# The same 13,990 operations of a two-layer transformer kernel in another written-out order

## The chip, the cores and the metric

The kernel runs on one core of a Trainium2 chip. Its metric is the device time of one execution in microseconds (us); lower is better. Five engines work side by side, each through its own instruction stream: TensorE (in profiles PE for the matmuls and PEld for the weight loads, which are instructions of the same stream), VectorE (DVE), ScalarE (ACT), GpSimd (POOL) and SyncE (SP). POOL and SP do little but issue transfers here. An engine takes its instructions in the order in which they stand in its stream, and semaphores make one engine wait for another.

## The reference

Four blocks follow one another on an input x of 2048 rows by 512 columns, in bf16: A, B, A, B, each added to x after a layer norm.

```
for s in range(64):                       # block A, segments of 32 rows
    h = concat(mem, x[32*s : 32*s+32])    # 8 memory rows + 32 rows
    q, k, v = h @ Wq, h @ Wk, h @ Wv      # 32 heads of 128
    p = softmax(mask(q @ k.T * scale))
    o = (p @ v) @ Wo
    mem = o[:8]                           # the next segment's memory
    outs.append(o[8:])

q, k, v = x @ wqkv                        # block B, linear attention, 32 heads of 16
kv, z = phi(k).T @ v, sum(phi(k))         # over all 2048 rows
out = (phi(q) @ kv) / (phi(q) @ z + 1e-6) @ wo
```

The 64 segments of block A can't run side by side: the memory rows that leave one segment enter the next. What doesn't depend on the memory (the rows' own output, the residual sums, all of block B's input side) can be done at any time after its inputs are there.

## The kernel before

Weights stay on the chip for the whole run. TensorE works with its array cut into four column strips of 32, so that nearly every step is a group of four matmuls, one a strip, and each of the four has its own weight load of 128 x 32. A group can do without the loads when the same weights are still in place; the helper `again` (its instruction is L2077) issues such matmuls.

One segment s of layer l is written as these steps, the names being the third part of the keys in the table:

- `kq0`, `kq1`: keys and queries of 16 heads each (`project`, matmuls of 512 columns at L2191 and L2077). Each result is copied out of PSUM by ACT or DVE (`evac`, L1954 and L1955) and turned by a DVE transpose (L2210).
- `v`: values, the same matmuls, copied out without a transpose.
- `mem0`, `mem1`: attention of the 8 memory rows, for 16 heads each. Number 0 and 1 are the score matmuls (L2325, L2317), 2 and 3 exponentials on ACT (L2332, L2336), 4 a product on DVE (L2340), 5 the matmuls of probabilities with values (L2353), then a reciprocal (L2358), a scaling (L2368 or L2370) and a transpose (L2360) on DVE and ACT.
- `out`: eight times eight matmuls of 256 columns with Wo (L2446), a copy on ACT or DVE (L1954, L1955), a sum on DVE (L2458).
- `next`: small f32 matmuls (L2476) that turn the eight new memory rows, and a copy into the next segment's input. `next` to `kq`, to `mem`, to `out`, to the next `next` is the recurrence that runs through all 64 segments.
- `x`: attention of the 32 rows (products at L2384, matmuls at L2396 and L2416), off that recurrence. `res`: the residual, with its transfers between partitions (`rows_out`). Every fourth segment adds `prep` (layer norm of the next 128 rows), `left` work for eight rows of each segment, `bi` (block B's input side) and, in layer 1, `bo` (the output side of the first block B, L2089). `lq` and `bl` are block B's queries and outputs at the two layers' ends.

What sets the order is a table, not the source's sequence of calls. Every operation has a key: layer, segment, step, number. `PLACE` (lines 16 to 1555) holds for each key one number, and a letter where ACT (`a`) or DVE (`v`) is chosen for an operation that either may do. `schedule` (L1681) sorts all operations by that number:

```
for nd in self.nodes:
    nd.t, nd.eng = when(nd.key, nd.engs)
seq = sorted(self.nodes, key=lambda n: (n.t, n.idx))
```

An engine's stream is the operations of that engine in the sorted order. PSUM banks are dealt out in the same order (the bank whose last user lies furthest back), and `finalize` (L1718) derives the semaphore waits; a wait rides on its instruction, and only an operation that needs two gets a further wait instruction ahead of it. So a change of the numbers alone changes the streams' order, the choice of ACT or DVE, the banks and the waits. The numbers are fixed in the file; the search that made them is not part of it. 

The program's TensorE stream has 43,597 matmuls and 39,357 weight loads. Instructions reach the engine by transfers of their own, on a queue that the profile lists as an instruction queue.

Of the kernel before, what the change touches and what calls it, by code (L numbers as in the profile page):

```python
# [16 lines left out]
    (0, -9, 'setup'): '3 0 1 4 5 7 8 9 10 11 12 13 14 0 6 2 15 16 18 19 20 21 23 26 30 33 36 41 43 45 49 0 59 0 68 100 101 94 99 104 190 212v 48 63a 0 108 113 117 121 126 92 258 0 0 0 0 0 0 0 0 0 0 0 0 0 0 0 0 0 0 0 0 0 0 0 0 0 0 0 0 0 0 0 0 0 0 0 0 0 0 0 0 0 0 0 0 0 0 0 0 0 0 0 0 0 0 0 0 0 0 0 0 0 0 0 0 0 0 0 0 0 0 0 0 0 0 0 0 0 0 0 0 0 0 0 0 0 80 88 0 0 0 0 0 0 0 0 0 0 0 0 0 0 0 0 0 0 0 0 0 0 0 0 0 0 0 0 0 0 0 0 0 0 0 0 0 0 0 0 0 0 0 0 0 0 0 0 0 0 0 0 0 0 0 0 0 0 0 0 0 0 0 0 0 0 0 0 0 0 0 0 0 0 0 0 0 0 0 0 0 0 0 0 0 0 0 0 0 0 0 0 55 0 0 62 0 0 72 84',  # L17
    (0, -5, 'ones'): '131 138 145 148',
    (0, -4, 'start'): '65a',
    (0, -3, 'spin'): '25 27 32 34 37 40 42 44',  # L20
    (0, -2, 'leftv'): '206 210 211 214 217v 222 226 225a 231 237',
    (0, -2, 'prep'): '24 28 29 31 38 46 50a 75v 93a 90v 91v',
    (0, -2, 'prepl'): '35 39 51 53 56 70 73v',
    (0, -1, 'spin'): '83 86 89 97',
    (0, 0, 'kq0'): '116 118 120 125 129 135 137 146 174v 181 159v 179',
    (0, 0, 'kq1'): '111 112 114 115 164 166 167 169 130a 194 172a 176a 187',
    (0, 0, 'ldqkv'): '281',
    (0, 0, 'lq'): '6434 6454 6456 6463 6470 6574 6583 6590',
    (0, 0, 'lx'): '6359',
    (0, 0, 'mem0'): '189 195 204 207 215 238 240 241v 246',  # L30
    (0, 0, 'mem1'): '193 197 203 208 224 247 252 254v 256',
    (0, 0, 'next'): '272 273 278v',
    (0, 0, 'out'): '251 253 255 257 259 261 263 265 268a 286',
    (0, 0, 'ql'): '186v 192a',
    (0, 0, 'sk'): '64 66 67 69 77v 82',
    (0, 0, 'sq'): '144 152 155 156 161a 165',
    (0, 0, 'v'): '218 227 228 230 234a 216 219 220 221 229a',
    (0, 0, 'x'): '233 262 242 249 250 264 266v 284 270 274 276 283 295v 322 243 275 317 356a 429',
    (0, 0, 'xl'): '22',
    (0, 1, 'kq0'): '282 285 287 288 290v 302 291a 298',  # L40
    (0, 1, 'kq1'): '289 293 294 296 292 297 300 301 299a 306 308a 304a 312',
    (0, 1, 'ldqkv'): '370',
    (0, 1, 'lq'): '6429 6451 6524 6527 6551 6556 6561 6582',
    (0, 1, 'mem0'): '309 310 314 336 318 325 328 329v 331',
    (0, 1, 'mem1'): '319 320 324 339 326 330 333 334a 338',
    (0, 1, 'next'): '359 360 361v',
    (0, 1, 'out'): '332 335 337 340 342 343 345 346 351a 358',
    (0, 1, 'ql'): '277a 269v',
    (0, 1, 'res'): '366 362',
    (0, 1, 'sk'): '76 78 79 81 85v 87',  # L50
    (0, 1, 'sq'): '133 134 154 158 168v 184',
    (0, 1, 'v'): '303 305 307 311 316a 313 315 321 323 327a',
    (0, 1, 'x'): '341 344 348 352 353 363 367a 375 354 355 357 372 378a 410 349 350 438 447a 457',
    (0, 2, 'kq0'): '365 369 373 381 383a 389 384v 392',
    (0, 2, 'kq1'): '376 379 380 382 385 386 387 390 388a 396 397a 393a 401',
    (0, 2, 'ldqkv'): '453',
    (0, 2, 'leftv'): '200 202 223 239 245a 260 279 271a 347 364',
    (0, 2, 'lq'): '6749 6761 6764 6765 6775 6787 6789 6797',
    (0, 2, 'lx'): '6433',
    (0, 2, 'mem0'): '398 399 403 427 406 413 416 417v 419',  # L60
    (0, 2, 'mem1'): '407 408 412 424 414 418 421 422a 426',
    (0, 2, 'next'): '448 449 451v',
    (0, 2, 'out'): '420 423 425 428 431 433 434 436 442a 474',
    (0, 2, 'prep'): '47 52 54 57 58 60 61a 98v 171v 140a 142a',
    (0, 2, 'ql'): '371v 377v',
    (0, 2, 'res'): '483 479',
    (0, 2, 'sk'): '74 122 123 124 127a 132',
    (0, 2, 'sq'): '173 178 183 185 188a 196',
    (0, 2, 'v'): '391 394 395 400 405a 402 404 409 411 415a',
    (0, 2, 'x'): '432 435 440 441 450 452 455v 459 444 445 446 458 461v 499 437 443 464 470a 525',  # L70
    (0, 3, 'kq0'): '454 456 460 462 465a 478 466v 472',
    (0, 3, 'kq1'): '463 467 475 477 468 469 471 473 484a 490 481a 476a 486',
    (0, 3, 'ldqkv'): '551',
    (0, 3, 'lq'): '6663 6666 6667 6672 6679 6697 6708 6717',
    (0, 3, 'mem0'): '487 488 493 511 496 502 505 506v 510',
    (0, 3, 'mem1'): '491 497 501 507 503 509 513 516a 520',
    (0, 3, 'next'): '536 538 542v',
    (0, 3, 'out'): '512 517 519 521 523 524 526 527 532a 535',
    (0, 3, 'ql'): '439v 430a',
    (0, 3, 'res'): '546 543',  # L80
    (0, 3, 'sk'): '71 95 96 128 136a 141',
    (0, 3, 'sq'): '139 143 162 177 198a 199',
    (0, 3, 'v'): '480 482 485 489 494a 492 495 498 500 504a',
    (0, 3, 'x'): '515 522 529 531 533 547 549v 552 528 530 540 554 556v 570 539 541 544 548a 589',
    (0, 4, 'kq0'): '545 550 553 555 558v 566 559a 563',
    (0, 4, 'kq1'): '557 564 567 569 560 561 562 565 574a 580 568a 572a 576',
    (0, 4, 'lq'): '6743 6751 6800 6821 6908 6934 6936 6941',
    (0, 4, 'lx'): '6689',
    (0, 4, 'mem0'): '577 578 582 605 585 592 597 599v 602',
    (0, 4, 'mem1'): '586 587 591 603 594 604 608 610v 613',  # L90
    (0, 4, 'next'): '628 629 632v',
    (0, 4, 'out'): '609 611 612 615 616 618 619 620 623a 627',
    (0, 4, 'ql'): '508v 534a',
    (0, 4, 'res'): '670 634 593 596 598 601 606 622 626 630 637a 641 646 644 658 650 662 656 651 663 705',
    (0, 4, 'sk'): '102 103 105 106 147v 149',
    (0, 4, 'sq'): '163 170 180 182 201a 205',
    (0, 4, 'v'): '571 573 575 579 584a 581 583 588 590 595a',
    (0, 4, 'x'): '617 614 625 633 635 640 643v 648 621 631 638 647 652v 673 624 636 716 720a 743',
    (0, 4, 'xl'): '17',
    (0, 5, 'kq0'): '639 642 645 649 657v 664 654a 669',  # L100
    (0, 5, 'kq1'): '661 666 667 671 653 655 659 660 674a 682 665a 668a 677',
    (0, 5, 'lq'): '6818 6848 6863 6866 6912 6919 6921 6927',
    (0, 5, 'mem0'): '675 676 683 680 691 696 702 704a 708',
    (0, 5, 'mem1'): '688 689 693 695 697 706 709 711v 714',
    (0, 5, 'next'): '736 737 739a',
    (0, 5, 'out'): '710 713 715 718 721 722 723 727 730a 740',
    (0, 5, 'ql'): '607a 600a',
    (0, 5, 'res'): '748 751',
    (0, 5, 'sk'): '107 109 110 119 153v 157',
    (0, 5, 'sq'): '150 151 160 175 209v 213',  # L110
    (0, 5, 'v'): '672 679 681 684 687a 678 686 690 692 699a',
    (0, 5, 'x'): '685 726 700 701 703 717 729v 745 731 732 735 786 794v 806 698 733 747 772a 876',
    (0, 6, 'bi'): '719 725 728 734 738 741 712 774 793 799 807 824 842 845 830a 1048 1106 1053 1174 817 822 828 838',
    (0, 6, 'kq0'): '742 746 750 758 761a 766 762v 770',
    (0, 6, 'kq1'): '765 769 771 773 754 768 777 779 776a 781 791a 787a 797',
    (0, 6, 'leftv'): '232 235 244 267 707a 749 752 753a 757 759',
    (0, 6, 'lq'): '6806 6808 6814 6816 6820 6832 6834 6842',
    (0, 6, 'lx'): '6740',
    (0, 6, 'mem0'): '788 792 798 800 801 805 808 810a 814',
    (0, 6, 'mem1'): '803 804 809 836 811 816 819 821a 825',  # L120
    (0, 6, 'next'): '843 844 847a',
    (0, 6, 'out'): '818 820 823 826 829 831 832 835 839a 849',
    (0, 6, 'prep'): '191 236 248 280 368 374 0 724v 518a 514v 537a',
    (0, 6, 'ql'): '780v 694v',
    (0, 6, 'res'): '854 852',
    (0, 6, 'v'): '760 783 784 789 795a 755 756 763 764 767a',
    (0, 6, 'x'): '802 840 812 813 815 827 858v 862 865 866 877 886 889v 899 919 927 931 934a 947',
    (0, 7, 'kq0'): '850 855 857 859 863a 881 868a 872',
    (0, 7, 'kq1'): '875 880 890 891 861 864 870 871 895a 902 874a 879a 883',
    (0, 7, 'lq'): '6798 6801 6803 6850 6918 6929 6930 6937',  # L130
    (0, 7, 'mem0'): '887 888 900 901 905 909 911 913a 917',
    (0, 7, 'mem1'): '896 908 912 921 915 918 922 924v 926',
    (0, 7, 'next'): '944 945 951v',
# [2806 lines left out]
```

## Time and profile before

| | us |
|---|---|
| median of three runs | 1510.44 |
| lowest and highest run | 1507.72, 1513.22 |
| the profiled execution | 1513.92 |
| its span | 1512.0 |
| mean granted TensorE clock | 0.998 |

The profile is of one execution; its span runs from the first to the last instruction, and the execution's time lies 1.9 us above it. Busy times are in us with their share of the span. A matmul's recorded end is modelled and includes the pipeline's tail, so that neighbouring matmuls overlap in the records, and a stream without holes shows in the distance between starts. In lists of waits a row says who waited for whom, then the sum, the number of waits and the longest; "issue" stands for idle time before an instruction that waited for nothing that the profile shows. In the chain of work that ended last, a row gives start, length and what ran.

### The profile page before, as it was taken

What the parts mean: (1) busy time and instruction counts of PE and PEld (TensorE: products, weight loads), DVE (VectorE), ACT (ScalarE), POOL (GpSimd) and SP (SyncE); (2) the same over time, 40 slices, a digit from 0 to 9 for tenths busy, and PEclk for the clock granted to TensorE, in tenths of its full rate; (3) what the DMA queues carried; (4) which work ended last, traced back from release to release, by engine and by line L of the source; (5) the groups of instructions that cost most, each with busy time, mean ns of one, the idle gap of its engine ahead of it and who ended that gap; (6) DMA issues with size and microseconds to landing.
All of it is one profiled execution on the core that took longest, in us unless ns stands there. A gap on an engine that the chain in (4) does not pass through costs nothing.

```text
span 1512.0 us, 90803 instructions
## 1 busy us (share of the span) xinstructions
PE 1458.4 (96%) x43597; PEld 835.8 (55%) x39357; DVE 1227.5 (81%) x4035; ACT 934.3 (62%) x2686; POOL 199.5 (13%) x398
## 2 busy tenths in 40 slices
PE   7999999999999999999999999999999999999998
PEld 3455555555565555555545555555555555555554
DVE  4788888888888788788878888788887888887777
ACT  2566556665665656565566767666666755666656
POOL 3011110111111011111111110111111011111010
PEclk9999999999999999999999999999999999999999
DMA  9310100100000010001310101011110111011034
GB/s 390 106 35 21 35 14 23 25 24 24 25 21 11 23 25 24 25 23 32 64 25 21 28 18 27 25 28 28 25 22 20 26 24 28 20 28 32 16 49 134
DMA packets 81639, 60.26 MB, mean 40 GB/s; under 512 B 64040, under 2 KB 74600, under 8 KB 79720
## 3 DMA queue, kind: packets, MB, share of 16 engines
q1 hardware_dynamic: 67944, 37.58, 9.7%
q0 software_dynamic: 13152, 16.75, 4.0%
q8 instruction: 324, 5.31, 1.5%
q14 instruction: 59, 0.48, 0.1%
q10 hardware_dynamic: 160, 0.14, 0.0%
HBM read 25.57 MB, written 11.67 MB: 25 GB/s over the span
## 4 chain that ended last, share of the span: by engine, by line
PE 81%; DVE 8%; DMA 5%; ACT 3%; issue 1%; SPq 1%; POOL 0%; DVEq 0%
PE pb L2191 36%; PE pb L2446 18%; PE pb L2077 13%; PE pb L2089 3%; PE pb L2396 2%; PE pb L2633 2%; DMA dx_sb<-y_sb 2%; PE pb L2353 2%; PE pb L2416 2%; ACT arena_sb L1954 2%; PE pb L2317 1%; PE pb L2476 1%; DVE arena_sb L2210 1%; DVE arena_sb L1955 1%; DMA Wk_sb<-in_A_Wk_dram 1%
## 5 line engine op out<-in xcount | busy, mean ns | idle before, releaser
L1954 ACT ACTIVATE arena_sb<-pb 128x512 bf16<-128x512 f32 (+3 forms) x1021 | 512.0, 529 | 285.7 <-PE pb L2077 125.5
L2191 PE MATMUL pb<-Wk_sb,arena_sb 128*32 128x512 bf16 x4192 | 363.5, 382 | 5.5 <-DVE arena_sb L1955 2.5
L2191 PE MATMUL pb<-Wv_sb,arena_sb 128*32 128x512 bf16 x4608 | 340.1, 379 | 1.2 <-ACT arena_sb L1954 0.9
L2446 PE MATMUL pb<-Wo_sb,arena_sb 128*32 128x256 bf16 x10368 | 328.2, 273 | 5.7 <-issue 1.3
L2210 DVE STREAM_TRANSPOSE arena_sb<-arena_sb 128x256 f32<-128x256 f32 x640 | 259.9, 426 | 43.0 <-ACT arena_sb L1954 37.6
L2446 PEld LDWEIGHTS pb<-Wo_sb,arena_sb 128*32 128x32 bf16 x10368 | 261.5, 97 | 43.5 <-DVE arena_sb L2360 16.7
L2191 PE MATMUL pb<-Wq_sb,arena_sb 128*32 128x512 bf16 x3088 | 257.5, 379 | 1.3 <-DVE arena_sb L1955 1.1
L1971 POOL DMA_DIRECT2D dx_sb<-y_sb x246 | 125.0, 512 | 921.6 <-DVE y_sb L2458 401.3
L2191 PEld LDWEIGHTS pb<-Wk_sb,arena_sb 128*32 128x32 bf16 x4192 | 118.7, 97 | 184.9 <-issue 95.4
L2368 ACT ACTIVATE arena_sb<-pb,arena_sb 128x128 bf16<-128x128 f32 x536 | 166.8, 368 | 71.3 <-DVE arena_sb L2403 27.6
L2077 PE MATMUL pb<-Wq_sb,arena_sb 128*32 128x512 bf16 x2032 | 203.1, 381 | 0.0
L2191 PEld LDWEIGHTS pb<-Wv_sb,arena_sb 128*32 128x32 bf16 x4608 | 120.9, 96 | 94.5 <-issue 13.0
L2370 DVE TENSOR_TENSOR arena_sb<-pb,arena_sb 128x384 bf16<-128x384 f32 (+2 forms) x366 | 153.8, 421 | 7.9
L1955 DVE CAST arena_sb<-pb 128x512 bf16<-128x512 f32 (+2 forms) x239 | 117.8, 495 | 48.3 <-PE pb L2077 33.2
L1954 ACT ACTIVATE outW_sb<-pb 128x256 f32<-128x256 f32 (+1 forms) x156 | 59.7, 383 | 140.9 <-PE pb L2446 112.9
L2191 PEld LDWEIGHTS pb<-Wq_sb,arena_sb 128*32 128x32 bf16 x3088 | 86.1, 97 | 84.8 <-issue 24.2
L2384 DVE TENSOR_TENSOR arena_sb<-arena_sb,wx_sb 128x640 bf16<-128x640 bf16 x256 | 117.9, 472 | 2.9 <-ACT arena_sb L2336 2.1
L2396 PE MATMUL pb<-arena_sb 128*32 128x130 bf16 x3072 | 105.9, 220 | 1.4 <-issue 1.2
L2406 DVE STREAM_TRANSPOSE arena_sb<-arena_sb 128x192 f32<-128x192 f32 x256 | 93.2, 364 | 15.2 <-ACT arena_sb L2368 13.3
L2458 DVE TENSOR_TENSOR y_sb<-pb,outW_sb 64x256 bf16<-64x256 f32 x162 | 68.7, 424 | 38.2 <-ACT outW_sb L1954 34.4
L2077 PE MATMUL pb<-Wk_sb,arena_sb 128*32 128x512 bf16 x928 | 91.8, 379 | 0.1
L2396 PEld LDWEIGHTS pb<-arena_sb 128*32 128x32 bf16 x3072 | 68.4, 96 | 30.7 <-issue 7.8
(128 smaller groups left out, 1808.5 us busy)
## 6 DMA issues: line engine op xcount, KB each, us to landing
Wk_sb<-in_A_Wk_dram SPq DMA_DIRECT2D x1, 4096.0 KB, 14.9
Wq_sb<-in_A_Wq_dram SPq DMA_DIRECT2D x1, 4096.0 KB, 24.2
Wv_sb<-in_A_Wv_dram SPq DMA_DIRECT2D x1, 4096.0 KB, 33.6
Wo_sb<-in_A_Wo_dram SPq DMA_DIRECT2D x8, 512.0 KB, 23.2
xs_scratch<-x_sb POOLq DMA_DIRECT2D x32, 128.0 KB, 2.2
pq_scratch<-arena_sb POOLq DMA_DIRECT2D x27, 128.0 KB, 2.3
x_sb<-xs_scratch POOLq DMA_DIRECT2D x16, 128.0 KB, 3.4
dx_sb<-y_sb SPq DMA_DIRECT2D x126, 12.0 KB
```

The lines of the kernel that those rows point to most:

```text
L1954: return e.activation(o() if callable(o) else o, i() if callable(i) else i, ACTF.Copy)
L1955: return e.tensor_copy(o() if callable(o) else o, i() if callable(i) else i)
L1971: add(eng, lambda e: e.dma_start(o, i), 0.55 if eng == "pool" else 0.66, reads=reads, writes=writes, dsem="%s%d" % (kind, k), lat=lat + (0 ...
L2077: return pe.add_instruction(mybir.InstMatmult(name=nc.get_next_instruction_name(), engine=mybir.EngineType.PE, ins=[pe.lower_ap(x), pe.low ...
L2191: r = pe.matmul(o, blk[:, c, :], w, start=(c == 0), stop=(c == 3), tile_position=(0, 32 * j))
L2210: add("dve", lambda v: v.transpose(dst, src(img[:, k, :].bitcast(F32))), 0.445, reads=[("img", k, h) for h in range(2)], writes=[dkey])
L2368: x = e.activation(o[:, u, :], i()[:, u, :], ACTF.Copy, scale=r[:, u:u + 1])
L2370: return e.tensor_tensor(o, i(), r.unsqueeze(2).to_broadcast([128, n, 128]), ALU.mult)
L2384: add("dve", lambda v, b=b: v.tensor_tensor(Px[:, b, :].rearrange("p (n j x) -> p n j x", n=20, j=4), PQ[:, r2, b, 64:224].rearrange("p (n ...
L2396: r = pe.matmul(pv.f32()[32 * i:32 * i + 32, 130 * k:130 * k + 130], cols(b, k, i), vimg[:, r2, 4 * b + i, :], start=True, stop=True, skip ...
L2406: add("dve", lambda v, b=b, k0=k0: v.transpose(oTb[:, s1, b, :, :, k0:k0 + 3].rearrange("p h j k q e -> p k (h j) (q e)").bitcast(F32), ox ...
L2446: r = pe.matmul(tl.f32()[32 * j:32 * j + 32, 0:256], oT[:, b, f, n, :, :, e], Wo_sb[:, 16 * b + 4 * n + 2 * f + e, 256 * d:256 * d + 256], ...
```

## The change

The table is replaced: 1,480 of its 1,521 lines within the part shown by the diff differ, and the keys and the number of entries of each are the same. No other line of the kernel changes, so each operation is the one it was, with the same shapes. The numbers come from a search that assumes a larger spacing in time between blocks of 256 TensorE instructions, and that takes each stretch of the order at its place in the instruction stream. Of 6,774 TensorE operations 4,081 stand at another place in their stream, half of all by one place or less and the furthest by 61; 322 copies and scalings go from DVE to ACT, and 297 from ACT to DVE. Two segments of layer 0, as they were and as they become:

```diff
@@ PLACE @@
-    (0, 21, 'mem0'): '2359 2361 2368 2396 2376 2380 2384 2386v 2388',
-    (0, 21, 'mem1'): '2371 2374 2379 2402 2383 2387 2389 2393v 2395',
+    (0, 21, 'mem0'): '2350 2351 2356 2383 2369 2375 2379 2386v 2388',
+    (0, 21, 'mem1'): '2377 2378 2381 2389 2384 2387 2394 2396v 2401',
...
-    (0, 21, 'out'): '2392 2394 2397 2400 2403 2405 2406 2409 2415a 2431',
+    (0, 21, 'out'): '2392 2395 2397 2399 2403 2404 2406 2407 2412a 2420',
...
-    (0, 44, 'kq1'): '4729 4737 4744 4745 4718 4721 4726 4727 4749a 4755 4731a 4734v 4739',
+    (0, 44, 'kq1'): '4738 4741 4742 4746 4730 4733 4734 4736 4750a 4756 4740a 4747v 4752',
...
-    (0, 44, 'mem1'): '4747 4762 4766 4777 4773 4778 4781 4783a 4787',
+    (0, 44, 'mem1'): '4766 4767 4771 4773 4774 4778 4782 4785a 4790',
...
-    (0, 44, 'v'): '4740 4743 4748 4750 4754a 4752 4758 4760 4763 4770a',
+    (0, 44, 'v'): '4735 4745 4755 4760 4765a 4749 4751 4753 4757 4768v',
```

The first eight numbers of `kq1` are its matmuls (four for the keys, four for the queries); of `mem1` the first two are the scores and the sixth the matmuls with the values. The last 478 TensorE operations (from layer 1's segment 56 on, 1395 us into the profile) keep their order; DVE's last 203 and ACT's last 133 keep theirs.

2948 rows, old and new, of the table PLACE are left out of this document.

## The prediction

> **What bounds the kernel now.** I read the page from the top, then the chain of work that ended last, then the waits.
>
> ```profile
> span 1512.0 us, 90803 instructions
> PE 1458.4 (96%) x43597; PEld 835.8 (55%) x39357; DVE 1227.5 (81%) x4035; ACT 934.3 (62%) x2686; POOL 199.5 (13%) x398
> PEclk9999999999999999999999999999999999999999
> q8 instruction: 324, 5.31, 1.5%
> PE 81%; DVE 8%; DMA 5%; ACT 3%; issue 1%; SPq 1%; POOL 0%; DVEq 0%
> ```
>
> TensorE is the bound: busy 96% of the span at the full granted clock, and 81% of the chain. No reordering can take its work away; it can only close holes. The holes that the page shows are 1512.0 - 1458.4 = 53.6 us. Two stretches, one of each layer, show where (length, then the busy time of PE, PEld, DVE, ACT and POOL, the clock, the DMA engines' share and GB/s):
>
> ```profile
> 300.00:400.00 100.00, 96.64 (x2976) 57.12 (x2692) 81.73 (x277) 60.31 (x176) 14.20 (x28) 1.00 0.08 20
> 1000.00:1100.00 100.00, 99.24 (x3045) 58.11 (x2737) 83.64 (x282) 66.25 (x198) 12.51 (x25) 1.00 0.12 27
> ```
>
> Layer 0 leaves 3.4 us in 100, layer 1 less than 1. Now the queue q8. 5.31 MB in 324 packets are 16,384 bytes each, and 43,597 + 39,357 = 82,954 instructions are 324 times 256: a packet of q8 brings a block of 256 TensorE instructions. Over the span that is a block every 1512.0 / 324 = 4.67 us. The chain between 494 and 500 us shows what happens when TensorE is faster than that:
>
> ```profile
> 496.40 0.17 PE pb L2476 x10
> 496.57 1.34 issue
> 497.91 0.22 PE pb L2476 x3
> ```
>
> In the middle of sixteen like matmuls TensorE stands for 1.34 us and waits for nothing. Counted along the stream (the 163 separate wait instructions included), this hole lies just where a block of 256 ends, and so do 29 others over 0.05 us, which all end 1.2 to 1.75 us after a packet of q8. The list of waits has the larger of them as PE's idle time (the first number is the sum), and two of the thirty stand for the rest:
>
> ```profile
> PE pb L2476 <- issue: 4.5, 3, 1.6
> PE pb L2446 <- issue: 1.3, 4, 0.4
> PE pb L2396 <- issue: 1.2, 3, 0.7
> PE pb L2416 <- issue: 0.6, 1, 0.6
> ...
> 219.46 0.23 PEld L2446 LDWEIGHTS pb<-Wo_sb,arena_sb 128*32 128x32 bf16 x12 [0.60 <-issue]
> 1471.60 0.12 PEld L2396 LDWEIGHTS pb<-arena_sb 128*32 128x32 bf16 x8 [0.39 <-issue]
> ```
>
> Their sum is at least 4.5 + 1.3 + 1.2 + 0.6 = 7.6 us and at most the chain's 1% of issue, 15 us (up to 1.5% if rounded, 23). From start to start of the matmuls, less the streaming time, I count 13.4 us in the thirty, and take that. The block before each lasted 3.0 to 4.4 us in most; in four it lasted 4.9 to 6.1, where waits for a semaphore stood at the block's start and the packet came late.
>
> **The change, part by part.** Nothing is added or removed, so the sum has only holes: at block ends, and where a matmul's input comes too late. For both I lay each order's matmuls end to end, at the distance at which they stream:
>
> ```profile
> 896.35 1.73 PE pb L2191 x32
> 901.00 2.18 PE pb L2446 x80
> 904.00 0.23 PE pb L2396 x16
> 81.60 0.10 PE pb L2317 x15
> ```
>
> A group of four takes 1.73 / 8 = 0.216 us with 512 columns, 2.18 / 20 = 0.109 with 256, 0.23 / 4 = 0.057 with 130, and 0.10 x 4 / 15 = 0.027 for the scores.
>
> *Block ends.* Cut every 256 instructions, the old order has 61 blocks of 323 under 3.4 us, which lack 23.2 us together; the new one 52, which lack 16.9 (27% less). That count leaves out the separate wait instructions. With them, at their old operations, every later cut shifts, by up to 162 instructions at the end, and the lack goes from 32.6 to 30.4 (7% less); with the old order's waits for inputs in the blocks too, it goes from 18.7 to 13.5 (28% less). The holes lie where the count with wait instructions puts them, so the benefit is between 7 and 28% of 13.4 us, 0.9 to 3.7. I take the middle, a gain of 2.3 us, since which operations need two waits in the new order is open.
>
> *Keys to scores.* Here an order can lack cover by a whole evacuation and transpose:
>
> ```profile
> 226.69 0.60 ACT L1954 ACTIVATE arena_sb<-pb 128x512 bf16<-128x512 f32 x1 [0.24 <-PE pb L2191]
> 227.65 0.44 DVE L2210 STREAM_TRANSPOSE arena_sb<-arena_sb 128x256 f32<-128x256 f32 x1
> 228.14 0.22 PE L2325 MATMUL pb<-arena_sb 128*32 128x64 bf16 x4 [1.29 <-DVE arena_sb L2210]
> ```
>
> A copy, a transpose and their hand-overs need some 1.3 us between the keys' last matmul (`kq1`, fourth number) and `mem1`'s scores. In segments 7 and 44 of layer 0 there were 0.22 and 0 us of other matmuls between; in the new order 1.86 and 1.64 (in 44, number 4745 to 4747 becomes 4746 to 4766). Over both layers the lack goes from 4.0 + 1.0 = 5.0 us to 1.0 + 0.3 = 1.4. That is a gain of at most 3.6; as some of these waits hide one another, and PE's idle rows hold 1.29 us of it in this one place, 2.8 is taken.
>
> *The recurrence.* The chain from 72 to 78 us shows its links, and the timeline one wait of them:
>
> ```profile
> 72.44 0.18 PE pb L2317 x16
> 72.65 0.23 ACT arena_sb L2332
> 72.91 0.29 DVE arena_sb L2340
> ...
> 74.06 1.96 PE pb L2446 x60
> 76.06 0.39 ACT outW_sb L1954
> 76.50 0.32 PE pb L2476 x16
> 77.04 0.20 DVE arena_sb L1955
> 77.28 0.40 PE pb L2191 x4
> ...
> 73.70 0.12 PEld L2353 LDWEIGHTS pb<-arena_sb 128*32 128x32 bf16 x8 [0.77 <-ACT arena_sb L1954]
> ```
>
> From `mem1`'s scores to its values (exponential, product) eight matmuls of 130 columns lie between there, 0.11 us, and the wait is 0.77 less the usual gap: it needs 0.87. From `out` to `next` it needs the matmul's tail, 0.39 and two hand-overs, 0.66. From `next` to the next keys, with a copy of 0.20 and a tail of near 0.2, 0.51. Over 126 segments, the lack of cover by these needs is: scores to values 9.5 us before and 12.3 after, +2.75 (in segment 21 of layer 0 the 0.54 us of cover become none: 2374, 2387 and 2378, 2387 are the numbers, and what lay between is gone); `out` to `next` 8.2 and 8.7, +0.5; `next` to keys 6.7 and 7.9, +1.2. The links from the values to `out` lack 43.5 us by a need of 1.17 before and 42.4 after, but the trace has only 13 us of holes there, so -1.1 x 13 / 43.5 = -0.3. Together +4.15 us. Both ends: none of it, where a late block of instructions fell on the same spot anyway, and 9 us, below.
>
> *Other engines.* 322 operations go to ACT and 297 to DVE, a net 25 away from DVE, which is busy 81%; most are copies of 0.2 to 0.6 us under TensorE's work. What makes that cost something is a copy that gets ahead of a product or a transpose that TensorE waits for: per place the 0.29 us of the product above. I cost it at 0 and put it into the range. Of POOL's 394 operations 139 move, by at most 4 places, of SP's 365 94, by at most 3; they carry residual rows and scratch copies, and POOL waits for DVE, not the other way round:
>
> ```profile
> POOL dx_sb L1971 <- DVE y_sb L2458: 401.3, 56, 13.1
> ```
>
> That cover gone, a transfer late would hold the layer norm of the next 128 rows; no row of PE's waits names it, so 0. From 1395 us on TensorE's order is the same and costs the same.
>
> [...]
>
> **Sum.** -2.3 - 2.8 + 4.15 = -0.95 us. The profiled execution took 1513.92, 3.5 above the median 1510.44, so against its own time 1512.97, and with the median's runs 1509.5.
>
> **Rivals.** *Fetch holes mostly go, faster.* If the spacing fits the chip, two thirds of 13.4 go (9 us), the keys give 3.6, and of the +4.15 half falls into blocks that had to be stretched in any case: -9 - 3.6 + 2.1 = -10.5, 1500. For it: the short blocks under 3.0 us fall from 25 to 16 in the count without wait instructions. Against: with them, 37 to 33.
>
> *The recurrence's cover decides, slower.* The links run through all 126 segments one after the other, and DVE, busy 81%, must serve the product in 0.87 us. 30 segments (24 before) have scores and values too close. If in each a moved DVE operation of 0.29 us stands ahead, that is 8.7 us more: -0.95 + 8.7 = +7.8, 1518. It decides from some 19 such places on (19 x 0.29 = 5.5). Against: layer 1 ran with 99% of PE busy at DVE's 83.64 us in 100.
>
> *The spacing doesn't do what it says.* The wait instructions shift the cuts, and as many holes stand at block ends, elsewhere: 0 - 2.8 + 4.15 = +1.35, 1512. [...]
>
> **How the numbers follow.** About 0.3%, 4.5 us, is what a measurement of this kernel can tell from no change: 1505.9 to 1515.0. The likeliest, gains and losses that cancel, gets 0.31, with a range of its own of 1506 to 1514; fewer fetch holes 0.34 and slower recurrence 0.28 are each a spread of sizes, mostly beyond 0.3%; no effect on the holes 0.07. A few of the spread cases end within: faster 0.33, same 0.40, slower 0.27. The predicted time is 1509.5 of the case in the middle. For 8 in 10 the range goes from a little under the faster rival (1500) to a little over the slower one (1518): 1497 to 1521.
>
> **What would show it.** Right: PE's rows with issue as the reason fall from 7.6 to about 6; the wait of 1.29 at L2325 is gone, and the idle rows of L2325 and L2317 shrink by 2 us or more; L2353's waits grow. Wrong: issue as large as before, or near 0; longer gaps at L2446 and L2353 in the windows of layer 0, with DVE as the reason, more than 4 us in all; a shift in the last 117 us, which no edit of TensorE's order explains.

## The result, and the profile after

The new order takes 1515.45 us (median of 22 runs, 1508.64 to 1518.58), the old one beside it 1509.8 (22 runs, 1506.12 to 1518.22). The ratio is 1.0032, with a 95% interval of 1.0022 to 1.0043: slower by 0.32% or, by this ratio, 4.8 us of 1509.8 (the medians themselves lie 5.65 apart). The prediction was no change, 1509.5. It is wrong in sign and in kind, though the time lies in its range.

The profile of the new order does not show a slower kernel. These are lines of its page, and two lines of its windows (length, then busy time of PE, PEld, DVE, ACT and POOL, clock, DMA share, GB/s).

```profile
span 1506.9 us, 90764 instructions
PE 1455.7 (97%) x43597; PEld 833.5 (55%) x39357; DVE 1224.2 (81%) x4010; ACT 936.7 (62%) x2690; POOL 199.8 (13%) x398
q8 instruction: 324, 5.31, 1.5%
PE 84%; DVE 7%; DMA 4%; ACT 2%; SPq 2%; issue 1%; POOL 0%; DVEq 0%
```

```profile
300.00:400.00 100.00, 97.27 (x3016) 58.37 (x2732) 81.43 (x274) 63.30 (x193) 13.93 (x27) 1.00 0.09 20
1000.00:1100.00 100.00, 99.17 (x3036) 56.70 (x2727) 82.07 (x269) 65.82 (x191) 12.09 (x24) 1.00 0.10 24
```

The span is 5.1 us shorter than that of before, layer 0 is a little denser in that stretch, layer 1 the same. This execution took 1508.64, the fastest of the 22 and 6.8 under their median, so it is not the one to explain a loss. Four more executions with the blocks at the same or nearly the same place, profiled for the experiments below, have spans of 1511.8, 1513.7, 1516.2 and 1513.1; the mean of the five is 1512.3. Four of the old order have 1512.0, 1512.2, 1513.1 and 1511.8, mean 1512.3. In the profiles the two orders are equal, in the timed runs they differ by 0.32%. Each profile is of one execution, and single executions of one kernel lie further apart than that: those of the old order's second run (`b_again`, below) go from 1505.79 to 1515.09.

The waits of PE as the list of each has them (sum, number, longest), first in the new order's first profile, then in a second of it, then in a second of the old order, and last one row of the old order's first:

```profile
PE pb L2353 <- DVE arena_sb L2340: 4.0, 10, 0.7
PE pb L2476 <- issue: 1.9, 2, 1.6
PE pb L2633 <- DMA arena_sb<-arena_sb: 1.4, 2, 0.7
PE pb L2396 <- issue: 0.9, 3, 0.5
PE pb L2325 <- DVE arena_sb L2210: 0.3, 1, 0.3
PE pb L2446 <- issue: 0.2, 1, 0.2
PE pb L2191 <- DVE arena_sb L1955: 2.0, 7, 0.3
PE pb L2191 <- ACT arena_sb L1954: 0.7, 2, 0.3
```

```profile
PE pb L2633 <- DMA arena_sb<-arena_sb: 4.3, 5, 1.6
PE pb L2476 <- issue: 2.5, 4, 0.9
```

```profile
PE pb L2476 <- issue: 4.5, 3, 1.6
PE pb L2446 <- issue: 1.7, 4, 0.7
PE pb L2396 <- issue: 1.1, 3, 0.5
PE pb L2633 <- DMA arena_sb<-arena_sb: 0.7, 2, 0.6
```

```profile
PE pb L2633 <- DMA arena_sb<-arena_sb: 0.3, 1, 0.3
```

Two things move: issue falls, as foretold, though further than to the 6 that was named (on the prediction's four lines 7.6 before and 1.9 + 0.9 + 0.2 = 3.0 after; over all profiles of the unmoved or nearly unmoved orders 6.0 to 7.7 and 3.0 to 5.1), and a row that the prediction had dismissed grows. L2633 is block B's input side, `bi`, and the DMA that it waits for is the transposing transfer of the normalised rows (L2117). The wait of 1.29 at L2325 is gone (it is not in the old order's second profile either, as will be seen), and L2353 behind its product waits no longer than before (4.0, and 4.3 then).

For a comparison line by line I took all holes from the traces: from start to start of PE's matmuls, less the time at which each shape streams, every hole over 0.04 us after the first 45 us. A hole at the place in the stream where a block of 256 ends is put to the block ends, all others to late inputs. Sums in us, means over the profiles named:

| holes | old order (4) | new order (5) | new order moved by 48, 112, 112 (3) |
|---|---|---|---|
| block ends | 17.6 | 12.6 | 9.2 |
| late inputs, all | 68.4 | 73.5 | 72.2 |
| scores, L2325 and L2317 | 5.6 | 3.2 | 2.2 |
| values, L2353 | 16.8 | 17.8 | 18.7 |
| `out`, L2446 | 13.6 | 12.7 | 12.4 |
| `next`, L2476 | 6.7 | 8.0 | 7.6 |
| projections, L2191 | 9.8 | 9.7 | 10.5 |
| `bi`, L2633 | 1.8 | 6.9 | 5.0 |
| `x`, L2396 and L2416 | 2.4 | 4.6 | 4.9 |

The last column is of an experiment below. The rows depend on the allowance for streaming: counted for each of the four strips by itself, with the prediction's distances, block ends come to 16.6, 11.8 and 8.8, and late inputs to 75.9, 80.5 and 76.2. The changes from column to column are the same in kind; a difference of 1 us in a row is not to be built on.

### The profile page after: what moved, and what is told of

The parts are those of the page before. It is cut to its first block, busy times and chain, and to the rows that moved or that the text cites. A ratio compares the mean times of both kernels' runs of the same rounds, so it can differ in the third digit from the quotient of the medians.

```text
span 1506.9 us, 90764 instructions
## 1 busy us (share of the span) xinstructions
PE 1455.7 (97%) x43597; PEld 833.5 (55%) x39357; DVE 1224.2 (81%) x4010; ACT 936.7 (62%) x2690; POOL 199.8 (13%) x398
## 4 chain that ended last, share of the span: by engine, by line
PE 84%; DVE 7%; DMA 4%; ACT 2%; SPq 2%; issue 1%; POOL 0%; DVEq 0%
PE pb L2191 37%; PE pb L2446 18%; PE pb L2077 14%; PE pb L2089 3%; PE pb L2396 2%; PE pb L2633 2%; SPq L1986 2%; PE pb L2353 2%; PE pb L2416 2%; PE pb L2476 2%; PE pb L2317 2%; DMA Wo_sb<-in_A_Wo_dram 1%; DVE arena_sb L2210 1%; ACT arena_sb L1954 1%; DMA arena_sb<-arena_sb 1%
## 5 line engine op out<-in xcount | busy, mean ns | idle before, releaser
L1954 ACT ACTIVATE arena_sb<-pb 128x512 bf16<-128x512 f32 (+3 forms) x1056 | 521.4, 522 | 277.1 <-PE pb L2077 136.0
L2191 PE MATMUL pb<-Wk_sb,arena_sb 128*32 128x512 bf16 x4192 | 363.5, 381 | 5.7 <-DMA Wk_sb<-in_A_Wk_dram 2.6
L2191 PE MATMUL pb<-Wv_sb,arena_sb 128*32 128x512 bf16 x4608 | 337.7, 378 | 1.2 <-DMA Wv_sb<-in_A_Wv_dram 1.1
L2446 PE MATMUL pb<-Wo_sb,arena_sb 128*32 128x256 bf16 x10368 | 328.9, 273 | 5.0 <-DVE arena_sb L2358 1.8
L2446 PEld LDWEIGHTS pb<-Wo_sb,arena_sb 128*32 128x32 bf16 x10368 | 261.4, 97 | 43.7 <-DVE arena_sb L2360 15.3
L2191 PE MATMUL pb<-Wq_sb,arena_sb 128*32 128x512 bf16 x3088 | 254.7, 379 | 0.5 <-DVE arena_sb L1955 0.2
L2191 PEld LDWEIGHTS pb<-Wk_sb,arena_sb 128*32 128x32 bf16 x4192 | 116.5, 97 | 185.9 <-issue 92.1
L2077 PE MATMUL pb<-Wq_sb,arena_sb 128*32 128x512 bf16 x2032 | 200.8, 379 | 0.0
L2368 ACT ACTIVATE arena_sb<-pb,arena_sb 128x128 bf16<-128x128 f32 x492 | 153.7, 370 | 68.3 <-DVE arena_sb L2403 26.6
L2191 PEld LDWEIGHTS pb<-Wv_sb,arena_sb 128*32 128x32 bf16 x4608 | 118.5, 96 | 94.6 <-issue 16.3
L2370 DVE TENSOR_TENSOR arena_sb<-pb,arena_sb 128x128 bf16<-128x128 f32 (+2 forms) x389 | 162.5, 419 | 8.3
L1955 DVE CAST arena_sb<-pb 128x512 bf16<-128x512 f32 (+2 forms) x206 | 106.2, 517 | 48.5 <-PE pb L2077 35.5
L2191 PEld LDWEIGHTS pb<-Wq_sb,arena_sb 128*32 128x32 bf16 x3088 | 85.9, 97 | 81.9 <-issue 24.0
L2396 PE MATMUL pb<-arena_sb 128*32 128x130 bf16 x3072 | 110.3, 220 | 1.4 <-issue 0.9
L2396 PEld LDWEIGHTS pb<-arena_sb 128*32 128x32 bf16 x3072 | 69.7, 96 | 32.6 <-issue 10.4
```

What stands on the lines that cost most here:

```text
L1954: return e.activation(o() if callable(o) else o, i() if callable(i) else i, ACTF.Copy)
L1955: return e.tensor_copy(o() if callable(o) else o, i() if callable(i) else i)
L2077: return pe.add_instruction(mybir.InstMatmult(name=nc.get_next_instruction_name(), engine=mybir.EngineType.PE, ins=[pe.lower_ap(x), pe.low ...
L2191: r = pe.matmul(o, blk[:, c, :], w, start=(c == 0), stop=(c == 3), tile_position=(0, 32 * j))
L2368: x = e.activation(o[:, u, :], i()[:, u, :], ACTF.Copy, scale=r[:, u:u + 1])
L2370: return e.tensor_tensor(o, i(), r.unsqueeze(2).to_broadcast([128, n, 128]), ALU.mult)
```

## The experiments

Two theories stood against each other. **Cover:** the new order's links lack cover (the recurrence, or `bi` behind its transposing transfer), so the loss goes with the order of the operations. **Place:** the loss hangs on which instructions a block of 256 happens to end at, so it goes when the same order is moved a few instructions along the stream. In all, 18 runs were made. Each ratio is to the old order run beside it on the same chip, with a 95% interval. The expectations name theories by letters, each explained where it first stands; F is in all of them the theory of the block ends, in changing words.

### Does it repeat, and in which half does it lie?

`a_again` and `b_again` are the new and the old order unchanged. `a0b1` has the new table up to number 6789 (layer 0 and the block B behind it, to 738 us), where both orders have done the same set of operations, and the old one after; `b0a1` is the other way round. One line of each half in `a0b1`, against the old table:

```diff
-    (0, 44, 'mem1'): '4747 4762 4766 4777 4773 4778 4781 4783a 4787',
+    (0, 44, 'mem1'): '4766 4767 4771 4773 4774 4778 4782 4785a 4790',
...
     (1, 20, 'mem1'): '9116 9117 9123 9124 9127 9130 9135 9137v 9140',
```

> The new order once more. Theory F (the holes at block ends vary from execution to execution, and the profiled one, 1506.9 us, had unusually few): a second profile near 1513 us, with more holes at block ends than the 7 us of the first profile, some 12. Theory W (the waits for inputs on the recurrence cost more in every execution): a second profile near 1513 us with holes at block ends again near 7 and the waits for inputs 4 to 5 us larger than the old order's. Both: a ratio near 1.003.

> The kernel before once more, for a second profile and for what a comparison gives where nothing differs. Both theories: 1.000 to the kernel before, within 0.0015. If one profile can stand for the median, this one's span lies near 1508 to 1512 us with holes at block ends of 10 to 16 us in all, as in the first profile.

> Layer 0 and its block B in the new order (up to 738 us), the rest in the old. The two orders have done the same operations at this cut, so the parts can be joined. If the loss of 0.32% is in layer 0 alone, 1.003; if in layer 1 alone, 1.000. Theory W, by the cover that I counted link by link (layer 0 about -0.5 us, layer 1 about +1.3), has it near 1.000. Theory F, by the lack of time in short blocks with every wait instruction counted (layer 0 9.2 to 4.2 us, layer 1 9.8 to 8.4), has it below 1.000 unless the executions vary.

> The other half: layer 0 in the old order, from 738 us on the new. If the parts add up, its ratio and that of the run before, each less 1, add up to 0.0032. Theory W: 1.001 to 1.003. Theory F: 0.999 to 1.000 by the counts.

| | ratio | 95% | median us |
|---|---|---|---|
| a_again | 1.0030 | 1.0018 to 1.0042 | 1513.21 |
| b_again | 1.0003 | 0.9988 to 1.0017 | 1510.12 |
| a0b1 | 1.0037 | 1.0025 to 1.0049 | 1514.13 |
| b0a1 | 1.0024 | 1.0008 to 1.0040 | 1512.56 |

The loss repeats. It has no half: each half alone loses about as much as the whole, and 0.37% + 0.24% = 0.61% is twice 0.30% (the intervals leave some 0.2% of doubt in the sum). Costs that belong to the operations of a stretch would add up. Theories W and F had both expected `a0b1` at or below 1.000. What a half also changes is the number of separate wait instructions ahead of the other half (154 in the new order's trace, 163 in the old one's), and with it where the blocks of the untouched half end: in the traces its instructions stand 22 places earlier in `a0b1`, and 22 later in `b0a1`, than in the kernel that it is taken from. That fits place; it doesn't show it.

### The same order, moved along the stream

Ahead of the first warm-up matmul, which runs before TensorE's wait for the first weights (2.0 us in the first profile of the old order, 2.6 in that of the new), some quads of small matmuls are added; a quad is four loads and four matmuls of 32 columns into a tile that the warm-up overwrites. Every later instruction moves by 8 places a quad, and nothing else changes. The edit for 48 (6 quads; in the others 1 for 8, 10 for 80, 14 for 112, 18 for 144, 24 for 192, 30 for 240, 32 for 256):

```diff
-            def mm(pe, tl=tl):
+            def mm(pe, tl=tl, first=(step == -3 and i == 0)):
                 x = one_sb[:, 0:128].unsqueeze(1).to_broadcast([128, 4, 128])
+                for u in range(6 if first else 0):
+                    for j in range(4):
+                        q = slice(32 * j, 32 * j + 32)
+                        pe.matmul(tl.f32()[q, 0:32], one_sb[:, q], one_sb[:, 0:32], start=True, stop=True, skip_group_check=True, tile_position=(0, 32 * j))
```

Later lines of these kernels stand four lower, so that L2476 becomes L2480.

> The new order, with 48 more small TensorE instructions in the first warm-up, before any weight has landed: they cost nothing there, but every later instruction stands 48 places later against the blocks of 256. Counted with all wait instructions and the covers, short blocks lack 18.0 us here, 12.5 with no shift. Theory F (block ends cost in every execution what the profile shows): 3 to 5 us slower than the new order, 1.005 to 1.007 to the kernel before, and more holes at block ends in the profile. Theory P (the timed executions don't pay at block ends what the profiled ones show): the same as the new order, 1.003, though its profile shows more holes.

> The same with 112 more instructions, the best place by the count: the short blocks lack 10.1 us. Theory F: 2 to 6 us faster than the run with 48, 1.001 to 1.003 to the kernel before. Theory P: the same as the run with 48, within 0.0015.

> The old order with 144 more: the lack falls from 19.0 to 13.2 us. Theory F: 0.997 to 0.998 to the kernel before, holes at block ends near 10 us in the profile instead of 14 to 15. Theory P: 1.000 within 0.0015.

> The old order with 192 more: the lack is 20.2 us. Theory F: 1.000 to 1.002, some 0.003 to 0.004 above the run with 144. Theory P: the same as the run with 144, within 0.0015.

A second set, on another chip, repeats the new order and the best place, and tries one place more of each:

> The new order with no shift, beside its shifted forms on one chip, since the shifted runs stood beside the old order alone. If the shift is what took the loss away, 1.003 again; if the chip did, 1.000.

> The new order with 112 small instructions ahead, once more. Theory F (the place of the block ends decides): 0.998 to 0.999 to the kernel before, 0.003 to 0.005 below the run without a shift. Theory C (the chips differ in how the two orders compare): within 0.0015 of the run without a shift.

> The new order with 240 more, that is, 16 less than a whole block. Counted, the short blocks lack 14.3 us (12.5 without a shift). If the timed executions stand at the places that the profile shows, 1.004 to the kernel before. If they stand some 64 instructions further on than the profiled ones, which would fit the three shifts measured so far, the lack is that of a shift of 48, 18.0, about the same as without a shift: 1.003 to 1.005. Both say not below 1.002; a value near 0.999 would say that a shift's amount does not matter and only its being there does.

> The old order with 80 more. At the profile's places the lack goes from 19.0 to 16.2 us: 0.998 to 0.999. If timed executions stand some 64 instructions further on, to 13.2: 0.996 to 0.998. If only the being there of a shift matters, as for the other theory, 1.001 to 1.002 as with 144 and 192.

A third set moves by a whole block, which brings every block end back to the same instruction, and by 8, nearly back:

> The new order with 256 small instructions ahead: every block of 256 ends at the same operation as without a shift, one block later. Theory F (the place of the block ends decides): 1.003 to the kernel before, as without a shift. Theory S (the added work at the start decides, whatever its amount): 0.999 to 1.001, as with 48 and 112.

> The old order with 256 ahead. Theory F: 1.000. Theory S: 1.001 to 1.002, as with 80, 144 and 192.

> The new order with 8 ahead. The lack of the short blocks changes by under 1.5 us against no shift, since a block end moves by four matmuls. Theory F: 1.002 to 1.004. Theory S: 0.999 to 1.001. Theory X (where holes fall is so sensitive that any shift draws a new time): anything from 0.998 to 1.004, and it would differ from the run with 256.

> The old order with 8 ahead. Theory F: 1.000 to 1.001. Theory S: 1.001 to 1.002. Theory X: the old order was an unusually short draw of its own, so 1.001 to 1.003.

| moved by | new order | 95% | span | old order | 95% | span |
|---|---|---|---|---|---|---|
| 0 | 1.0030 | 1.0018 to 1.0042 | 1511.8 | 1.0003 | 0.9988 to 1.0017 | 1512.2 |
| 0 | 1.0035 | 1.0020 to 1.0051 | 1513.7 | | | |
| 256 | 1.0047 | 1.0029 to 1.0065 | 1516.2 | 1.0010 | 0.9998 to 1.0023 | 1513.1 |
| 8 | 1.0021 | 1.0008 to 1.0033 | 1513.1 | 1.0003 | 0.9990 to 1.0016 | 1511.8 |
| 48 | 0.9999 | 0.9986 to 1.0012 | 1507.8 | | | |
| 80 | | | | 1.0012 | 1.0001 to 1.0024 | 1508.6 |
| 112 | 0.9985 | 0.9971 to 0.9998 | 1507.6 | | | |
| 112 | 1.0001 | 0.9991 to 1.0011 | 1507.4 | | | |
| 144 | | | | 1.0012 | 1.0000 to 1.0024 | 1508.8 |
| 192 | | | | 1.0021 | 1.0005 to 1.0038 | 1512.6 |
| 240 | 1.0014 | 1.0005 to 1.0023 | 1510.0 | | | |

Moved by 48 or 112 instructions, with every operation in the new order, the loss is gone; moved by 256 it is back. So the loss hangs on the place of the block ends; the new order alone does not bring it. At 240, 16 short of a block, half of it is there. The old order stands, with 0 and 8, at the best of the places tried for it, and loses 0.1 to 0.2% at three others, by intervals that begin at or just above 1. At its best place the new order equals the old one: 0.9985 did not repeat (1.0001), so neither order, at any place tried, is shown to beat the old kernel.

Which place is good was not foretold. The sizes expected came from a count of blocks that are too short, and that count had 48 as worse than no move (1.005 to 1.007; measured 0.9999), the old order as faster with 144 and 80 (0.996 to 0.999; measured 1.0012 twice), and the new one with 240 as no better than 1.002 (measured 1.0014).

The chain of the new order moved by a whole block, where a block ends among the sixteen matmuls of `next`:

```profile
498.11 0.22 PE pb L2480 x13
498.33 1.92 issue
500.25 0.21 PE pb L2480 x2
```

In the one moved by 112 this place has no hole, and another `next` has one:

```profile
274.43 0.17 PE pb L2480 x7
274.60 1.41 issue
276.00 0.26 PE pb L2480 x9
```

The new order unmoved (`a_again`) runs through that `next` without a hole, as its chain shows:

```profile
275.03 0.24 PE pb L2476 x16
```

Inside the `next` of that segment (at 493 to 500 us) the five profiles moved by 0, 8 or 256 have a hole of 0.7 to 2.4 us, the three moved by 48 or 112 have none. In the one at 274 us it is the other way round: none against 1.6 and 1.5 with 112. All in all these three have 3.4 us less at block ends and 1.3 less at late inputs (the table above; 3.0 and 4.3 by the other count); the spans, 1512.3 and 1507.6 on average, differ by 4.7. Between the timed ratios lie mostly 0.3 to 0.5%, 5 to 7 us (0.2% for the run moved by 8).

That it is the holes in `next` for which the timed runs pay is not shown, and the old order speaks against it. Its lists have 4.5, 4.5 and 4.3 us of issue at `next` unmoved, again unmoved and moved by 256, three holes each time. Moved by 80 or 144 it has no such row, its holes at block ends fall (by the other count from 16.6 to 7.6 and 10.8), and so do its spans, but its timed runs get no faster (1.0012). The new order moved by 240 has no such row either, and 1.0014.

### More cover ahead of block B's inputs

L2633 had grown from 1.8 to 6.9 us of holes. Both orders' timelines of the same step in layer 0, first a second profile of the old order:

```profile
403.24 0.38 DVE L2133 TENSOR_SCALAR arena_sb<-x_sb,st_sb 128x512 bf16<-128x512 bf16 x1
403.65 1.20 SPq L2117 DMA_TRANSPOSE arena_sb<-arena_sb  x1
404.24 0.55 POOL L1971 DMA_DIRECT2D x_sb<-in_A_x_dram  x1 [1.72 <-DVE arena_sb L2406]
404.78 0.54 POOL L1971 DMA_DIRECT2D xn_scratch<-arena_sb  x1
407.74 0.40 PE L2633 MATMUL pb<-arena_sb 128*32 128x512 bf16 x4
```

and of the new one (`a_again`):

```profile
402.30 0.41 DVE L2133 TENSOR_SCALAR arena_sb<-x_sb,st_sb 128x512 bf16<-128x512 bf16 x1
402.74 1.20 SPq L2117 DMA_TRANSPOSE arena_sb<-arena_sb  x1
403.01 0.55 POOL L1971 DMA_DIRECT2D xn_scratch<-arena_sb  x1 [1.40 <-DVE arena_sb L2340]
403.55 0.54 POOL L1971 DMA_DIRECT2D x_sb<-in_A_x_dram  x1
408.47 0.40 PE L2633 MATMUL pb<-arena_sb 128*32 128x512 bf16 x4 [1.58 <-DMA arena_sb<-arena_sb]
```

The old order's matmul comes 407.74 - 403.65 = 4.1 us after the transfer's issue and finds it landed. In the new order TensorE is ready after 5.73 - 1.58 = 4.15 us, no earlier, yet the transfer takes 5.7. Two POOL transfers stand the other way round beside it, and the one with scratch is issued 0.27 us after the transpose, where it was 1.13. That they delay it is not shown: in two of the other four profiles of the new order it had landed after some 4.0 us (3.9 in the first). At two other steps (359 and 624 us) TensorE came 5.6 to 6.0 us after the issue in the four profiles of the old order; in nine of ten cases of the new one it is ready after 3.6 to 4.3, and it waits up to 1.7. But it was no work that made TensorE come later there in the old order. A block ends in the `next` just ahead of these matmuls, here in the first profile of before:

```profile
363.73 0.29 PE pb L2476 x15
364.02 1.56 issue
365.59 0.20 PE pb L2476
365.79 0.23 PE pb L2633 x4
```

Moved by 80 or 144, the old order's TensorE is there after 4.0 to 4.1 us. So a hole at a block end can be the cover of a transfer. Nor is the wait at L2633 the new order's own: with TensorE's order untouched, the old one waits there 4.2, 4.5 and 2.0 us when it is moved by 80, 144 and 192, against 0.3 to 0.7 at 0, 8 and 256, and transfers that took 3.2 us to land then take up to 5.9.

`a_cover` gives cover back as work. In 17 of block B's 30 places its first matmuls go 0.1 to 0.9 us further back, behind key and query projections of the next segment, so that between layer norm and matmul stands at least what the old order had, 5.6 us more in all; `a_cover112` is the same, moved by 112. One place:

```diff
-    (0, 50, 'bi'): '5274 5284 5287 5291 5294 5298 5279 5344 5347 5352 5406 5432 5437 5439 5426a 5652 5705 5683 5743 0 0 0 5317',
-    (0, 50, 'kq0'): '5353 5355 5357 5361 5373a 5388 5366a 5383',
+    (0, 50, 'bi'): '5274 5284 5287 5291 5294 5298 5279 5353 5354 5355 5406 5432 5437 5439 5426a 5652 5705 5683 5743 0 0 0 5317',
+    (0, 50, 'kq0'): '5350 5352 5357 5361 5373a 5388 5366a 5383',
```

> The new order, in which in 17 of the 30 places block B's first matmuls stand 0.1 to 0.9 us later behind projections that depend on nothing of theirs, so that there is at least as much TensorE work between the layer norm and them as in the old order (5.6 us more over the 17). No shift. Theory T (the transposing transfer's lost cover is a large part of the loss): TensorE's waits for that transfer at L2633 fall from 4 us or so to under 2, and the ratio to the kernel before goes from 1.003 to between 1.000 and 1.0015. Theory F alone (only the block ends cost): the waits fall, and the ratio stays at 1.002 to 1.004, since another wait comes last there.

> Both: the cover given back and 112 small instructions ahead. The new order with 112 alone gave 0.9985 and 1.0001. Theory T: the two add up, 0.996 to 0.998, a version that beats both kernels. Theory F alone: 0.999 to 1.000 as with the shift.

Measured: 1.0107 (1.0087 to 1.0127) and 1.0092 (1.0075 to 1.0110), 1524.93 and 1523.64 us. Both theories missed this: they had 1.000 to 1.004 for the first and 0.996 to 1.000 for the second. The waits of `a_cover` say why:

```profile
PE pb L2633 <- DMA arena_sb<-arena_sb: 0.6, 2, 0.4
PE pb L2191 <- ACT arena_sb L1954: 5.8, 13, 1.0
PE pb L2191 <- DVE arena_sb L1955: 5.7, 10, 1.2
```

The wait for the transfer falls to 0.6 (in the new order's profiles 1.4 to 5.3), and the projections now wait for the new memory's copy: 5.8 + 5.7 = 11.5, against 0.7 + 2.0 in the list of the new order above. Block B's matmuls had been the cover between `next` and the next keys; pulling the projections ahead of them uncovered the recurrence, which is the longer chain. By lines, L2633's holes fall to 3.5, L2191's rise from 9.7 to 20.9, L2476's from 8.0 to 11.1, and late inputs in all from 73.5 to 83.5. What the 5 us at L2633 cost the timed runs is not measured by this: the edit paid for them with a dearer wait. Issuing the transposes earlier, with TensorE's order kept, was not tried.

## Why the prediction was wrong

*What bounds it.* Right: TensorE, at 96 to 97% of the span and a granted clock of 0.998 and 0.999 (first profiles of the old and the new order), and only holes can move.

*Block ends, -2.3.* This is the step that failed. It counted how many blocks of each order are short (its 3.4 us lies where the closest packets of q8 do: the ten closest start 3.28 to 3.41 us apart in the first profile of the old order, 3.34 to 3.47 in that of the new), took "between 7 and 28% of 13.4 us" and "the middle". In the profiles the share came out right, 17.6 to 12.6 being 28% less, the upper end, though of a larger sum (-5.0). But the count gives an order one value, and the timed runs give it a spread: the same order costs from about nothing (48, 112) to 0.30 to 0.47% (0, 256) by the place of its cuts. What the count leaves out is what a cut falls on: in the profiles a cut in the middle of one `next` makes a hole of 0.7 to 2.4 us, and none when it is moved. Which cuts the timed runs pay for stays open. This spread of 5 to 7 us was never set as a term, and the wait instructions that set the place were left "open". It belonged in the sum as some 3 us either way, half the spread (an estimate after the fact). The 4.8 us lost are about the whole of it: of the places tried, the old order stands at one of its best and the new one at its worst, which is luck and no worth of either order.

*From the profile to the median.* The second failing step: the sum was made against one profiled execution and carried over to the median runs. In the profiles it came near, 1512.3 and 1512.3 where the sum said -0.95. The timed runs do not follow them. The old order's profiled executions moved by 0, 8 or 256 took 0.9 to 4.1 us more than the median of the same kernel (1514.2 and 1510.12 for `b_again`), the new order's 0.3 more to 1.0 less in four of five and 6.8 less in the first; moved by 80, 144 and 192 the old order's took 0.7 to 2.2 less. So `b_shift80`, whose span is 3.6 us shorter than that of `b_again`, is not faster in the timed runs (1.0012 and 1.0003). Why is open. Chance is not excluded: each of these is one execution, and those of `b_again` alone lie up to 9 us apart. The shifts show that the place decides in timed runs; which holes these have, the profiles do not settle.

*Keys to scores, -2.8.* Right in size: L2325 and L2317 went from 5.6 to 3.2, -2.4. But the wait of 1.29, the prediction's example, was misread. The transpose ahead of those scores stood on DVE behind a residual sum that waited for its transfer (first row below, of the old order's first profile). In a second profile of the same order (the other rows) the transfer lands earlier, the transpose runs before the copy shown in the prediction has begun, so that the copy is no link of this chain, and TensorE waits 0.17:

```profile
227.31 0.42 DVE L2525 TENSOR_TENSOR x_sb<-x_sb,dx_sb 128x512 bf16<-128x512 bf16 x1 [1.40 <-DMA dx_sb<-y_sb]
```

```profile
225.84 0.42 DVE L2525 TENSOR_TENSOR x_sb<-x_sb,dx_sb 128x512 bf16<-128x512 bf16 x1 [0.28 <-DMA dx_sb<-y_sb]
226.18 0.44 DVE L2210 STREAM_TRANSPOSE arena_sb<-arena_sb 128x256 f32<-128x256 f32 x1
226.34 0.60 ACT L1954 ACTIVATE arena_sb<-pb 128x512 bf16<-128x512 f32 x1 [0.24 <-PE pb L2191]
226.67 0.21 PE L2325 MATMUL pb<-arena_sb 128*32 128x64 bf16 x4 [0.17 <-DVE arena_sb L2210]
```

One profile of the new order (`a_plain2`) has the same wait again, 0.82 behind 0.93 at the sum. DVE's waits for these transfers come to 2.9 to 4.9 us in the old order's four profiles and to at most 2.5 in the new order's five; how much of the -2.4 is theirs and how much is cover is not shown.

*The recurrence, +4.15.* Direction right, size too large: values +1.0 for 2.75, `next` +1.3 for 0.5, projections -0.1 for 1.2, `out` -0.9 for -0.3; together +1.3. Lack of cover by a fixed need overstates what a stretch costs that waits a little later in any case (this is argued, not shown). What `a_cover` did to L2191 shows that the link is real where it is cut.

*Other engines and moved transfers, 0.* Wrong in the profiles: L2633 +5.1 us. The argument, made for late residual transfers, was that "no row of PE's waits names it". It left out the transposing transfers: for them the list of before has a row, at 0.3, and a wait near zero does not tell that there is cover to spare. The old order, merely moved, waits there as long, so this term goes with the place too. The `x` matmuls, 0 in the sum, took 2.2 more.

By terms, then, -5.0 - 2.4 + 1.3 + 5.1 + 2.2 = +1.2, with -1.1 at L2089 about the 0 that the profiles' spans show: gains and losses that cancel, as the sum had it, only not those.

*The rivals.* Fetch holes that mostly go, 1500: no, though the holes at block ends fell by 28% in the profiles. The recurrence's cover, 1518: the time is near, the mechanism is not, since the loss goes with a shift that leaves the order, and with it the work that covers each link, as it is. The spacing that doesn't do what it says, 1512, with 7% of the chance: nearest in mechanism, since "as many holes stand at block ends, elsewhere", but it put the net at nothing and not at some us either way.

## What to carry to other kernels

Where the profile has holes at the ends of blocks of instructions (here blocks of 256, one in 4.67 us on average, with 17.6 us of holes at their ends in the old order and 12.6 in the new), a reordering is judged only after the same order has been timed at several places in the stream; a few idle instructions at the start do it (here 8 to 256), and tell the order's worth (here none that shows) from the luck of its place (here 0.3 to 0.5%). A transfer whose waiter hardly waits may be a link at its limit (L2633 waited 0.3 to 0.7 us in the old order at 0, 8 and 256, and up to 4.5 at other places), and moving its waiter or its neighbours is to be priced. Before work is put ahead of a waiting instruction, ask what that instruction itself was covering: 5.6 us of cover given to one wait cost 0.7 to 1% at another. A wait of one profile is to be sought in a second before it is priced: the 1.29 us were one execution's late transfer.

## What the runs showed of the hardware

Separate wait instructions count in the blocks. In the first profiles of the old and the new order, after the first 45 us, TensorE's instructions start over 0.41 us apart 13 and 5 times where the later one waits for no semaphore. All 18 places lie a multiple of 256 from one another in their stream if its 163 or 154 wait instructions are counted; if not, the remainders by 256 drift from 172 to 34 and from 162 to 58 along it. Each of these holes ends 1.2 to 1.6 us after the landing of the packet of q8 that came last before it.

In the old order holes of over 1 us at `next` stood from profile to profile until the stream was moved, and came back after 256: its lists have three unmoved, unmoved again and moved by 256 (4.5, 4.5 and 4.3 us in sum, the longest 1.6 in each), and none with 80 or 144.

The transposing transfer of 128 rows landed 3.9 us after its issue in the first profile of the new order and 5.7 after it in `a_again`, at the same step (402 us).
